# First-chunk q projection of a two-layer attention and SwiGLU kernel: tile 1 averaged by halves, tile 3 transposed by DMA, q's second half in passes of 128 tokens, wo in four loads

## The chip, the core and the metric

The kernel runs on one core of one Trainium2 chip. The metric is device time in microseconds (us) of one execution, as a median over fast runs. Engines are named as in the profile: PE is TensorE's matmul, PEld its weight loads, DVE is VectorE, ACT is ScalarE, POOL is GpSimd, SP is SyncE, which issues most DMAs. L347 is line 347 of the kernel's source. A bank is a buffer that PE's matmuls write into (in PSUM); copying it out is called evacuating it. In the profile's names, x is the input, xn a normalised or centred tile, xnT its transpose, slot a buffer for weights, wo the weights of the output projection, and oT the attention's output.

## The reference, cut to what matters

```
x = x + A(layernorm(x), wqkv, wo)        # attention, 32 heads, window of 8 keys 2 apart
x = x + B(layernorm(x), w1, w3, w2)      # SwiGLU, F = 3584
x = x + A(layernorm(x), wqkv, wo)        # the same weights again
x = x + B(layernorm(x), w1, w3, w2)
```

x is 2048 tokens by 1024, bf16. The kernel works on 4 chunks of 512 tokens, each of 4 tiles of 128 tokens.

## The kernel before

The program records operations (engine, estimated duration, what is read and written) and a list scheduler puts them in order for each engine. For PE it picks among lanes; lane 1 is attention's output projection:

```
def place(self, n_banks=8, rate=330e3):
    ...
            if e == "PE":
                cands = []
                for k, ops in lanes.items():
                    if heads[k] < len(ops) and waiting[ops[heads[k]]] == 0:
                        cands.append(ops[heads[k]])
                times = [(max(free[e], ready_at[o], bank_time(o)), -o.lane, o.seq, o) for o in cands]
    ...
```

The program then gives each engine its instructions in exactly this order, whatever the real durations are.

The edit is in the function that does the first chunk's q projection. Tiles 0 and 1 are centred, transposed on PE and projected while weight rows still arrive; their scaling is applied later. Tiles 2 and 3 are normalised, transposed on PE and projected as q's second half. Tiles 0 and 1 are then also normalised and transposed by DMA, for k and v:

```
def q_first():
    ...
    for j in range(2, TPC):                       # tiles 2 and 3
        stats(j, [("ce", 1, 0)]); root(j, j + 1); apply(j)
        transposed(xn[j], ..., xnT[b][:, :, j * P:(j + 1) * P], ...)     # on PE, through PSUM
    for j in range(2):                            # tiles 0 and 1, for k and v
        ...
        dma(256, xnT[b][:, :, j * P:(j + 1) * P], xn[j][:], ..., transpose=True)
    ...
    wslots[1] = q_weights(1, "s")                 # k: two loads of 1 MB, ready to issue at once
    ...
```

The output projection adds into x, and the feed-forward stage of the same chunk starts from that x. It has to normalise it and to transpose it by DMA before its first matmul:

```
def b_stage(l, c):
    b = ln(c)          # statistics, normalise, 4 DMA transposes into xnT
    ...                # every first matmul reads all of xnT
```

Of the kernel before, what the change touches and what calls it, by code (L numbers as in the profile page):

```python
# [9 lines left out]
ALU = mybir.AluOpType  # L10
# [146 lines left out]
def kernel(  # L157
# [11 lines left out]
    nc = tc.nc  # L169
    P = 128  # L170
# [77 lines left out]
    def dve(dur, emit, reads, writes, cls=2, **kw):  # L248
        return pr.add("DVE", dur, emit, reads, writes, cls, **kw)

    def act(dur, emit, reads, writes, cls=0, **kw):
        return pr.add("ACT", dur, emit, reads, writes, cls, **kw)
# [167 lines left out]
    def transposed(src, keys, dst, dkeys, pieces=((0, 4, "DVE"), (4, 8, "ACT"))):  # L420
        for k0, k1, eng in pieces:
            n = k1 - k0
            add, fn, dur = ((dve, nc.vector.tensor_copy, 0.15 + n * 0.0675) if eng == "DVE" else
                            (act, nc.scalar.copy, 0.2 + n * 0.0975))
            a = Acc()

            def tr(op, a=a, k0=k0, n=n):
                pt = bank[a.bank][:].bitcast(BF16)
                for k in range(n):
                    nc.tensor.transpose(pt[:, k * P:(k + 1) * P], src[:, (k0 + k) * P:(k0 + k + 1) * P], ident[:])  # L430
            tro = pr.add("PE", 0.0625 * n, tr, [keys[k0 // 4], "ident"], [], takes=[a], lag=0.17, lane=2)

            def emit(op, a=a, k0=k0, k1=k1, n=n, fn=fn):
                pt = bank[a.bank][:].bitcast(BF16)
                fn(dst[:, k0:k1, :], pt[:, 0:n * P].rearrange("p (k t) -> p k t", k=n))
            evac(add, dur, emit, tro, [], dkeys[k0:k1], a, cls=-9)

    def q_first():
# [6 lines left out]
        for kk in range(4):  # L445
# [5 lines left out]
        rows[2](7)  # L451
        b, q, stats, root, apply = ln(0, first=True)
        ce = hT[:, 8:16, :]
        dve(0.77, lambda _: nc.vector.tensor_scalar(xn[2][:, 0:512], x_sb[0][:, 0:512], 1.0 / D, 0.0, op0=ALU.mult,
                                                    op1=ALU.add, accum_out=mean[:, 0:1]),
            [("x", 0, 0)], [("xn", 2), ("mean", 0)], -9)
        act(0.82, lambda _: nc.scalar.activation(xn[3][:, 0:512], x_sb[0][:, 512:1024], ACTF.Copy, scale=1.0 / D,
                                                 accum_out=part[:, 0:1]), [("x", 0, 1)], [("xn", 3), ("part", 0)], -9)
        rows[2](6, queue="AQ", after=[("part", 0)])
        act(1.25, lambda _: nc.scalar.activation(xn[3][:], x_sb[1][:], ACTF.Copy, scale=1.0 / D,  # L460
                                                 accum_out=mean[:, 1:2]), [("x", 1, 0), ("x", 1, 1)],
            [("xn", 3), ("mean", 1)], -9)
        for j in range(2):
            for h in range(2):
                c0 = 512 * h
                if j == 0:
                    dve(0.31, lambda _, c0=c0: nc.vector.tensor_scalar(
                        xn[0][:, c0:c0 + 512], x_sb[0][:, c0:c0 + 512], mean[:, 0:1], part[:, 0:1], op0=ALU.subtract,
                        op1=ALU.subtract), [("x", 0, 0), ("x", 0, 1), ("mean", 0), ("part", 0)],
                        [("xn", 0), ("xn", 0, h)], -9)  # L470
                else:
                    dve(0.31, lambda _, c0=c0: nc.vector.tensor_scalar(  # L472
                        xn[1][:, c0:c0 + 512], x_sb[1][:, c0:c0 + 512], mean[:, 1:2], None, op0=ALU.subtract),
                        [("x", 1, 0), ("x", 1, 1), ("mean", 1)], [("xn", 1), ("xn", 1, h)], -9)
            transposed(xn[j], [("xn", j, h) for h in range(2)], ce[:, :, j * P:(j + 1) * P],
                       [("ce", j, k) for k in range(KT)],
                       ((0, 2, "DVE"), (2, 4, "DVE"), (4, 8, "ACT")) if j == 0 else ((0, 4, "DVE"), (4, 8, "ACT")))
        dve(0.16, lambda _: nc.vector.tensor_tensor(mean[:, 0:1], mean[:, 0:1], part[:, 0:1], op=ALU.add),
            [("mean", 0), ("part", 0), ("ce", 1, 0)], [("mean", 0)], -9)
        for j in range(2, TPC):  # L480
            stats(j, [("ce", 1, 0)])
            root(j, j + 1)
            apply(j)
            transposed(xn[j], [("xn", j)] * 2, xnT[b][:, :, j * P:(j + 1) * P],
                       [("xnT", b, j, k // 4) for k in range(KT)])
        for j in range(2):
            act(1.25, lambda _, j=j: nc.scalar.activation(sgt[j][:].rearrange("p a b -> p (a b)"), x_sb[j][:],
                                                          ACTF.Square, bias=mean[:, j:j + 1], scale=-1.0,
                                                          accum_out=part[:, j:j + 1]),
                [("x", j, 0), ("x", j, 1), ("mean", j)] + [("ce", 1, KT - 1)],  # L490
                [("part", j), ("sgt", j, 0), ("sgt", j, 1)], -8)
            act(0.3, lambda _, j=j: nc.scalar.activation(sd[q][:, j:j + 1], part[:, j:j + 1], ACTF.Sqrt, bias=epst[:],
                                                         scale=1.0 / D),
                [("part", j), "eps"], [("sd", q, j)], -8, table="sqrt")
            dve(0.16, lambda _, j=j: nc.vector.reciprocal(rstd[q][:, j:j + 1], sd[q][:, j:j + 1]), [("sd", q, j)],
                [("rstd", q, j)], 0)
            dve(0.5, lambda _, j=j: nc.vector.tensor_scalar(xn[j][:], x_sb[j][:], mean[:, j:j + 1],
                                                            rstd[q][:, j:j + 1], op0=ALU.subtract, op1=ALU.mult),
                [("x", j, 0), ("x", j, 1), ("mean", j), ("rstd", q, j), ("xn", TPC - 1)],
                [("xn", j)] + [("xn", j, h) for h in range(2)], 0)  # L500
            dma(256, xnT[b][:, :, j * P:(j + 1) * P], xn[j][:], [("xn", j)], [("xnT", b, j)], 0, transpose=True)
# [6 lines left out]
        def store(pa, op, j0):  # L508
            for g in range(4):
                evac(act, 0.59, lambda _, a=pa[g], g=g: nc.scalar.copy(  # L510
                    hT[:, 2 * g:2 * g + 2, j0 * P:(j0 + 2) * P],
                    bank[a.bank][:].rearrange("p (m t) -> p m t", m=2)), op[g], [],
                    [("hT", 2 * g + m, j) for m in range(2) for j in (j0, j0 + 1)], pa[g])
# [12 lines left out]
        store(pa, [op] * 4, 0)  # L526
        pa = [Acc() for _ in range(4)]
        ops = []
        for g in range(4):
            lk = [[q_lhs(wslots[0], kk, m)[0] for kk in range(KT)] for m in (2 * g, 2 * g + 1)]  # L530

            def emit(op, g=g, lk=lk, pa=pa):
                for m in range(2):
                    for kk in range(KT):
                        nc.tensor.matmul(bank[pa[g].bank][:, m * 2 * P:(m + 1) * 2 * P], lhsT=lk[m][kk],  # L535
                                         rhs=xnT[b][:, kk, 2 * P:4 * P], start=(kk == 0 and m == 0),
                                         stop=(kk == KT - 1), skip_group_check=True)
            ops.append(pr.add("PE", 16 * 0.1092, emit,
                              [("w", i, k) for i in wslots[0][0] for k in range(4)] +
                              [("xnT", b, j, h) for j in (2, 3) for h in range(2)],  # L540
                              [], takes=[pa[g]], lag=0.17))
        store(pa, ops, 2)
        for m0 in range(0, KT, 2):
            dma(256, spill_view(0, 0, m0, 0), hT[:, m0:m0 + 2, :],
                [("hT", m, j) for m in (m0, m0 + 1) for j in range(TPC)], [("d", 0, 0, 0, m0)], 1)
# [6 lines left out]
        for which, key, tile_ in ((1, "kT", kT), (2, "vT", vT)):  # L552
            dve(0.11, lambda _, tile_=tile_: nc.vector.memset(tile_[:, :, 0:HALO], 0.0), [], [(key, "h")], 1)
            q_tile(0, 0, which, wslots[which], b, (key, tile_))
        for t0, t1_ in ((0, 2), (2, 4), (4, 6), (6, 7), (7, 8)):
            dma(256 * (t1_ - t0), wo[:, t0:t1_, :], wo_v[:, t0:t1_, :], [("d", 0, 2, 0, 6)], [("wo", t0)], 3)
        stage_no[0] += 1

# [24 lines left out]
    def t_stage(l, half):  # L583
# [54 lines left out]
        for j in range(TCH // P):  # L638
            n = tok0 // P + j
            for hh in range(2):  # L640
                a = Acc()
                op = mm8(a, [(oT[oh][:, t, j * P:(j + 1) * P], wo[:, t, hh * 512:(hh + 1) * 512]) for t in range(KT)],
                         True, True, [("oT", oh, t) for t in range(KT)] + [("wo", t) for t in (0, 2, 4, 6, 7)], lane=1)
                xs = x_sb[n][:, hh * 512:(hh + 1) * 512]
                evac(dve, t1(512), lambda _, xs=xs, a=a: nc.vector.tensor_tensor(xs, xs, bank[a.bank][:], op=ALU.add),  # L645
                     op, [("x", n, hh)], [("x", n, hh)], a)
# [126 lines left out]
```

## Time and profile before

| | before |
|---|---|
| median of 3 runs | 1614.96 us |
| span of the profiled run | 1613.1 us |
| PE busy | 99% of the span |
| PE waits, whole run | 1.4 us, all before 7 us |
| first matmul of k (L347) | 21.49 us |

The span runs from the first instruction to the last. A line of the timeline gives the start, the length, the engine, the line, the operation, output and input, the number of instructions merged, and in brackets the idle time before it with what ended it. The lines themselves stand in the prediction.

### The profile page before, as it was taken

Reading aid. Unit: us, or ns where it says so; the run is one execution under the profiler, and the core shown is the slowest. Engines: PE = TensorE matmul, PEld = TensorE weight load, DVE = VectorE, ACT = ScalarE, POOL = GpSimd, SP = SyncE. Lnnn points to the kernel's source line nnn. Section 1 sums busy time; section 2 is a strip of 40 time slices with the busy share of each in tenths; the row PEclk is TensorE's granted clock in tenths of the full one; section 3 lists DMA queues with packets and bytes.
Section 4 is the critical chain, followed back from the end, with each engine's and each line's share of the span. In section 5 each row is a group of like instructions: output and inputs, shape, how many; then the busy total and the mean of one; then the engine's idle time right before and its main releaser. Section 6 shows DMA issues by size and latency. Waiting matters only on the chain.

```text
span 1613.1 us, 19082 instructions
## 1 busy us (share of the span) xinstructions
PE 1601.3 (99%) x7463; PEld 762.7 (47%) x7610; DVE 1122.3 (70%) x1906; ACT 329.6 (20%) x526; POOL 5.3 (0%) x28
## 2 busy tenths in 40 slices
PE   9999999999999999999999999999999999999999
PEld 7555544444444444444444444444444444444444
DVE  5899888988889888898898729884299831211211
ACT  5423322021201222113311032110321101101110
POOL 1000000000000000000000000000000000000000
PEclk9999999999999999999999999999999999999999
DMA  9834755495548764858545487365873464454451
GB/s 321 228 105 151 221 166 171 127 227 158 171 141 253 194 186 137 216 164 251 176 131 163 157 248 228 121 176 174 254 220 118 160 179 156 144 177 149 156 167 42
DMA packets 350649, 285.80 MB, mean 177 GB/s; under 512 B 72288, under 2 KB 344928, under 8 KB 350560
## 3 DMA queue, kind: packets, MB, share of 16 engines
q1 hardware_dynamic: 350128, 283.94, 58.8%
q8 instruction: 59, 0.97, 0.2%
q10 hardware_dynamic: 432, 0.66, 0.1%
q14 instruction: 30, 0.25, 0.1%
HBM read 238.94 MB, written 29.36 MB: 166 GB/s over the span
## 4 chain that ended last, share of the span: by engine, by line
PE 99%; issue 1%; DMA 0%; ACT 0%; DVE 0%; ACTq 0%
PE bank L347 98%; PE bank L535 0%; PE bank L521 0%; DMA x<-in_A_x_dram 0%; PE bank L430 0%; ACT L281 0%; DVE xn L472 0%; ACT xn L460 0%; DVE x L700 0%; ACTq L460 0%
## 5 line engine op out<-in xcount | busy, mean ns | idle before, releaser
L347 PE MATMUL bank<-xnT,slot 128*128 128x512 bf16 x4955 | 1088.7, 379 | 5.3
L347 PEld LDWEIGHTS <-slot 128*128 128x128 bf16 x5056 | 518.2, 102 | 572.9
L347 PE MATMUL bank<-slot,hT 128*128 128x512 bf16 (+2 forms) x1812 | 387.3, 372 | 1.9
L670 DVE TENSOR_TENSOR hT<-sg,bank 128x512 bf16<-128x512 bf16 x224 | 153.4, 685 | 214.4 <-PE bank L347 194.9
L265 DVE TENSOR_TENSOR scr<-scr 128x1024 bf16<-128x1024 bf16 (+3 forms) x576 | 293.4, 539 | 2.0
L347 PEld LDWEIGHTS <-hT 128*128 128x128 bf16 x1848 | 178.5, 98 | 208.7
L668 ACT ACTIVATE sg<-bank 128x512 bf16<-128x512 f32 x224 | 133.7, 597 | 660.5 <-PE bank L347 608.8
L265 DVE TENSOR_TENSOR scr<-qT,kT 128x2048 bf16<-128x2048 bf16 x128 | 154.1, 1219 | 73.3 <-DMA kT<-qkv_d 71.0
L405 ACT CAST sgt<-bank 128x512 bf16<-128x512 f32 x184 | 107.3, 585 | 315.2 <-PE bank L347 300.3
L265 DVE TENSOR_TENSOR scr<-pA,vT 128x2048 bf16<-128x2048 bf16 x128 | 152.5, 1220 | 0.3
L700 DVE TENSOR_TENSOR x<-x,bank 128x512 bf16<-128x512 bf16 (+1 forms) x66 | 43.9, 670 | 121.5 <-PE bank L347 121.4
L347 PE MATMUL bank<-wo,oT 128*128 128x512 bf16 x502 | 112.6, 379 | 0.6
L313 DVE BATCH_NORM_STATS2 st<-x 128x6 f32<-128x512 bf16 x124 | 81.8, 681 | 11.9 <-DMA x<-in_A_x_dram 11.4
L347 PEld LDWEIGHTS <-oT 128*128 128x128 bf16 x512 | 50.1, 98 | 60.3
L645 DVE TENSOR_TENSOR x<-x,bank 128x512 bf16<-128x512 bf16 x64 | 43.9, 687 | 37.0 <-PE bank L347 35.8
L320 ACT ACTIVATE sd<-mv,epst 128x4 f32<-128x4 f32 (+1 forms) x17 | 5.1, 297 | 172.4 <-DVE mv L316 172.1
L628 DVE STREAM_TRANSPOSE pA<-pB 128x2048 bf16<-128x2048 bf16 x16 | 37.0, 2310 | 0.5
L605 DVE STREAM_TRANSPOSE pB<-pA 128x2048 bf16<-128x2048 bf16 x16 | 37.0, 2310 | 0.5
L668 ACT ACT_TABLE_LOAD x20 | 25.7, 1283 | 56.2 <-PE bank L347 56.0
L265 DVE TENSOR_TENSOR pA<-scr 128x256 bf16<-128x256 bf16 x128 | 35.9, 286 | 0.4
L265 DVE TENSOR_TENSOR oT<-scr 128x256 bf16<-128x256 bf16 x128 | 33.9, 288 | 0.1
L327 DVE TENSOR_SCALAR xn<-x,mv,rstd 128x1024 bf16<-128x1024 bf16 x62 | 30.7, 541 | 3.5 <-DMA xnT<-xn 3.4
(61 smaller groups left out, 209.0 us busy)
## 6 DMA issues: line engine op xcount, KB each, us to landing
slot<-in_B_w_dram SPq DMA_DIRECT2D x160, 1024.0 KB, 5.9
slot<-in_A_wqkv_dram SPq DMA_DIRECT2D x28, 1024.0 KB, 5.1
qkv_d<-sgt SPq DMA_DIRECT2D x92, 256.0 KB, 3.3
qT<-qkv_d SPq DMA_DIRECT2D x16, 512.0 KB, 5.7
slot<-in_B_w_dram SPq DMA_DIRECT2D x16, 512.0 KB, 5.7
kT<-qkv_d SPq DMA_DIRECT2D x14, 544.0 KB, 6.7
vT<-qkv_d SPq DMA_DIRECT2D x14, 544.0 KB, 4.9
out_dram<-x SPq DMA_DIRECT2D x31, 128.0 KB, 4.3
```

The lines of the kernel that those rows point to most:

```text
L265: return lambda _: nc.vector.tensor_tensor(o, a, b, op=op)
L313: dve(0.67, lambda _, hh=hh: nc.vector.bn_stats(st[q][:, j, hh, :], x_sb[n][:, hh * 512:(hh + 1) * 512]), [("x", n, hh)] + list(after), [( ...
L320: act(0.3, lambda _: nc.scalar.activation(sd[q][:, j0:j1], mv[q][:, j0:j1, 1], ACTF.Sqrt, bias=epst[:]), [("mv", q, j) for j in range(j0, ...
L327: dve(0.5, lambda _: nc.vector.tensor_scalar(xn[j][:], x_sb[n][:], mv[q][:, j, 0:1], rstd[q][:, j:j + 1], op0=ALU.subtract, op1=ALU.mult), ...
L347: nc.tensor.matmul(bank[a.bank][:, 0:ncol], lhsT=w, rhs=r, start=first and i == 0, stop=last and i == n - 1)
L405: evac(act, 0.59, lambda _, a=a, i=i, m=m: nc.scalar.copy(sgt[i][:, m % 2, :], bank[a.bank][:]), op, [], [("sgt", i, m % 2)], a)
L605: dve(2.31, lambda _: nc.vector.transpose(psmT[:].rearrange("p c d -> p (c d)"), psm[:].rearrange("p w s -> p (w s)")), allA, ["pB"])
L628: dve(2.31, lambda _: nc.vector.transpose(At[:].rearrange("p w s -> p (w s)"), AeT[:].rearrange("p c d -> p (c d)")), ["pB"], allA)
L645: evac(dve, t1(512), lambda _, xs=xs, a=a: nc.vector.tensor_tensor(xs, xs, bank[a.bank][:], op=ALU.add), op, [("x", n, hh)], [("x", n, hh) ...
L668: evac(act, 0.6, lambda _, i=i, a=ag: nc.scalar.activation(sg[i][:], bank[a.bank][:], ACTF.Silu), og, [], [("sg", i)], ag, table="silu")
L670: evac(dve, t1(512), lambda _, i=i, a=au, f=f: nc.vector.tensor_tensor(hT[:, f, :], sg[i][:], bank[a.bank][:], op=ALU.mult), ou, [("sg", i ...
L700: evac(dve, t1(cn), lambda _, xs=xs, a=a, cn=cn: nc.vector.tensor_tensor(xs, xs, bank[a.bank][:, 0:cn], op=ALU.add), op, [("x", n, hh)], [ ...
```

## The change

The intent is to take work off PE in the first 21 us, where it waits and where it does transposes instead of matmuls. Tile 1's mean is formed half on DVE and half on ACT. Tile 3 is transposed by DMA instead of on PE, and so that PE need not wait for it, q's second half goes over tile 2 first and over tile 3 after that. wo comes in four loads instead of five.

```
-        for j in range(2): ...        # tile 1: one ACT sum over 1024, one subtraction operand
+        for j in range(2):
+            dve(0.77, ... tensor_scalar(xn[2][:, 0:512], x_sb[j][:, 0:512], 1.0 / D, ..., accum_out=mean[:, j:j + 1]) ...)
+            act(0.82, ... activation(xn[3][:, 0:512], x_sb[j][:, 512:1024], ..., accum_out=part[:, j:j + 1]) ...)
             ...
-                       ((0, 2, "DVE"), (2, 4, "DVE"), (4, 8, "ACT")) if j == 0 else ((0, 4, "DVE"), (4, 8, "ACT")))
+                       ((0, 2, "DVE"), (2, 4, "DVE"), (4, 8, "ACT")))
         ...
-            transposed(xn[j], [("xn", j)] * 2, xnT[b][:, :, j * P:(j + 1) * P], ...)
+            if j == 2:
+                transposed(xn[j], [("xn", j)] * 2, xnT[b][:, :, j * P:(j + 1) * P], ...)
+            else:
+                dma(256, xnT[b][:, :, j * P:(j + 1) * P], xn[j][:], ..., transpose=True)
         ...
-        for g in range(4):                       # 16 matmuls of 256 columns each
+        for j in (2, 3):
+            for g in range(4):                   # 16 matmuls of 128 columns each
         ...
-        for t0, t1_ in ((0, 2), (2, 4), (4, 6), (6, 7), (7, 8)):
+        for t0, t1_ in ((0, 2), (2, 4), (4, 6), (6, 8)):
             dma(256 * (t1_ - t0), wo[:, t0:t1_, :], ...)
```

More of the change, by code (lines that the diff above doesn't have):

```diff
@@ L453, in q_first @@
         ce = hT[:, 8:16, :]
-        dve(0.77, lambda _: nc.vector.tensor_scalar(xn[2][:, 0:512], x_sb[0][:, 0:512], 1.0 / D, 0.0, op0=ALU.mult,
-                                                    op1=ALU.add, accum_out=mean[:, 0:1]),
-            [("x", 0, 0)], [("xn", 2), ("mean", 0)], -9)
-        act(0.82, lambda _: nc.scalar.activation(xn[3][:, 0:512], x_sb[0][:, 512:1024], ACTF.Copy, scale=1.0 / D,
-                                                 accum_out=part[:, 0:1]), [("x", 0, 1)], [("xn", 3), ("part", 0)], -9)
@@ L459, in q_first @@
-        rows[2](6, queue="AQ", after=[("part", 0)])
-        act(1.25, lambda _: nc.scalar.activation(xn[3][:], x_sb[1][:], ACTF.Copy, scale=1.0 / D,
-                                                 accum_out=mean[:, 1:2]), [("x", 1, 0), ("x", 1, 1)],
-            [("xn", 3), ("mean", 1)], -9)
-        for j in range(2):
-            for h in range(2):
-                c0 = 512 * h
-                if j == 0:
-                    dve(0.31, lambda _, c0=c0: nc.vector.tensor_scalar(
-                        xn[0][:, c0:c0 + 512], x_sb[0][:, c0:c0 + 512], mean[:, 0:1], part[:, 0:1], op0=ALU.subtract,
-                        op1=ALU.subtract), [("x", 0, 0), ("x", 0, 1), ("mean", 0), ("part", 0)],
-                        [("xn", 0), ("xn", 0, h)], -9)
-                else:
-                    dve(0.31, lambda _, c0=c0: nc.vector.tensor_scalar(
-                        xn[1][:, c0:c0 + 512], x_sb[1][:, c0:c0 + 512], mean[:, 1:2], None, op0=ALU.subtract),
-                        [("x", 1, 0), ("x", 1, 1), ("mean", 1)], [("xn", 1), ("xn", 1, h)], -9)
+        for j in range(2):
+            dve(0.77, lambda _, j=j: nc.vector.tensor_scalar(xn[2][:, 0:512], x_sb[j][:, 0:512], 1.0 / D, 0.0,
+                                                             op0=ALU.mult, op1=ALU.add, accum_out=mean[:, j:j + 1]),
+                [("x", j, 0)] + [("ce", 0, 2)] * j, [("xn", 2), ("mean", j)], -9)
+            act(0.82, lambda _, j=j: nc.scalar.activation(xn[3][:, 0:512], x_sb[j][:, 512:1024], ACTF.Copy,
+                                                          scale=1.0 / D, accum_out=part[:, j:j + 1]),
+                [("x", j, 1)], [("xn", 3), ("part", j)], -9)
+            if j == 0:
+                rows[2](6, queue="AQ", after=[("part", 0)])
+            for h in range(2):
+                dve(0.31, lambda _, j=j, c0=512 * h: nc.vector.tensor_scalar(
+                    xn[j][:, c0:c0 + 512], x_sb[j][:, c0:c0 + 512], mean[:, j:j + 1], part[:, j:j + 1],
+                    op0=ALU.subtract, op1=ALU.subtract), [("x", j, 0), ("x", j, 1), ("mean", j), ("part", j)],
+                    [("xn", j), ("xn", j, h)], -9)
@@ L475, in q_first @@
             transposed(xn[j], [("xn", j, h) for h in range(2)], ce[:, :, j * P:(j + 1) * P],
                        [("ce", j, k) for k in range(KT)],
-                       ((0, 2, "DVE"), (2, 4, "DVE"), (4, 8, "ACT")) if j == 0 else ((0, 4, "DVE"), (4, 8, "ACT")))
-        dve(0.16, lambda _: nc.vector.tensor_tensor(mean[:, 0:1], mean[:, 0:1], part[:, 0:1], op=ALU.add),
-            [("mean", 0), ("part", 0), ("ce", 1, 0)], [("mean", 0)], -9)
+                       ((0, 2, "DVE"), (2, 4, "DVE"), (4, 8, "ACT")))
@@ L480, in q_first @@
+        dve(0.16, lambda _: nc.vector.tensor_tensor(mean[:], mean[:], part[:], op=ALU.add),
+            [("mean", j) for j in range(2)] + [("part", j) for j in range(2)] + [("ce", 1, 0)],
+            [("mean", j) for j in range(2)], -9)
         for j in range(2, TPC):
@@ L483, in q_first @@
             apply(j)
-            transposed(xn[j], [("xn", j)] * 2, xnT[b][:, :, j * P:(j + 1) * P],
-                       [("xnT", b, j, k // 4) for k in range(KT)])
+            if j == 2:
+                transposed(xn[j], [("xn", j)] * 2, xnT[b][:, :, j * P:(j + 1) * P],
+                           [("xnT", b, j, k // 4) for k in range(KT)])
+            else:
+                dma(256, xnT[b][:, :, j * P:(j + 1) * P], xn[j][:], [("xn", j)], [("xnT", b, j, h) for h in range(2)],
+                    0, transpose=True)
         for j in range(2):
@@ L489, in q_first @@
                                                           accum_out=part[:, j:j + 1]),
-                [("x", j, 0), ("x", j, 1), ("mean", j)] + [("ce", 1, KT - 1)],
+                [("x", j, 0), ("x", j, 1), ("mean", j), ("xnT", b, 2, 1) if j else ("ce", 1, KT - 1)],
                 [("part", j), ("sgt", j, 0), ("sgt", j, 1)], -8)
@@ L528, in q_first, with emit @@
         ops = []
-        for g in range(4):
-            lk = [[q_lhs(wslots[0], kk, m)[0] for kk in range(KT)] for m in (2 * g, 2 * g + 1)]
-            def emit(op, g=g, lk=lk, pa=pa):
-                for m in range(2):
-                    for kk in range(KT):
-                        nc.tensor.matmul(bank[pa[g].bank][:, m * 2 * P:(m + 1) * 2 * P], lhsT=lk[m][kk],
-                                         rhs=xnT[b][:, kk, 2 * P:4 * P], start=(kk == 0 and m == 0),
-                                         stop=(kk == KT - 1), skip_group_check=True)
-            ops.append(pr.add("PE", 16 * 0.1092, emit,
-                              [("w", i, k) for i in wslots[0][0] for k in range(4)] +
-                              [("xnT", b, j, h) for j in (2, 3) for h in range(2)],
-                              [], takes=[pa[g]], lag=0.17))
-        store(pa, ops, 2)
+        for j in (2, 3):
+            for g in range(4):
+                lk = [[q_lhs(wslots[0], kk, m)[0] for kk in range(KT)] for m in (2 * g, 2 * g + 1)]
+                def emit(op, g=g, lk=lk, pa=pa, j=j):
+                    for m in range(2):
+                        t0 = m * 2 * P + (j - 2) * P
+                        for kk in range(KT):
+                            nc.tensor.matmul(bank[pa[g].bank][:, t0:t0 + P], lhsT=lk[m][kk],
+                                             rhs=xnT[b][:, kk, j * P:(j + 1) * P],
+                                             start=(kk == 0 and m == 0 and j == 2), stop=(kk == KT - 1),
+                                             skip_group_check=True)
+                ops.append(pr.add("PE", 16 * 0.0558, emit,
+                                  [("w", i, k) for i in wslots[0][0] for k in range(4)] +
+                                  [("xnT", b, j, h) for h in range(2)], [], takes=[pa[g]], lag=0.17))
+        store(pa, ops[4:], 2)
         for m0 in range(0, KT, 2):
@@ L642, in t_stage @@
                 op = mm8(a, [(oT[oh][:, t, j * P:(j + 1) * P], wo[:, t, hh * 512:(hh + 1) * 512]) for t in range(KT)],
-                         True, True, [("oT", oh, t) for t in range(KT)] + [("wo", t) for t in (0, 2, 4, 6, 7)], lane=1)
+                         True, True, [("oT", oh, t) for t in range(KT)] + [("wo", t) for t in (0, 2, 4, 6)], lane=1)
                 xs = x_sb[n][:, hh * 512:(hh + 1) * 512]
```

## The prediction

> **What bounds the kernel now.** I read the page of the profile first: the busy shares, then the chain that ended last.
>
> ```profile
> span 1613.1 us, 19082 instructions
> PE 1601.3 (99%) x7463; PEld 762.7 (47%) x7610; DVE 1122.3 (70%) x1906; ACT 329.6 (20%) x526; POOL 5.3 (0%) x28
> PE 99%; issue 1%; DMA 0%; ACT 0%; DVE 0%; ACTq 0%
> ```
>
> TensorE (PE) carries 99% of the span and of the chain; no other engine is near it. So the next view is the list of waits of PE over the whole run, which has three lines in all:
>
> ```profile
> PE bank L285 <- PEq L757: 0.8, 1, 0.8
> PE bank L430 <- DVE xn L472: 0.4, 1, 0.4
> PE bank L521 <- DMA slot<-in_A_wqkv_dram: 0.2, 1, 0.2
> ```
>
> Columns: who waited for whom, total us, times, longest. All of it lies in the first 7 us. From the first matmul of k (line 347, at 21.49 us) PE runs to the end without a wait. The change touches only the first chunk's q projection, before that matmul, and the loads of wo. So the whole question is: **at what time does the first L347 matmul start?** Whatever that start moves, the end moves, unless a new wait appears later.
>
> The timeline of the first 60 us gives the start of every PE stage (start us, length us, engine, line):
>
> ```profile
> 5.19 0.61 PE L521 MATMUL bank<-hT,slot 128*128 128x128 bf16 x8
> 5.96 0.62 PE L521 MATMUL bank<-hT,slot 128*128 128x128 bf16 x8 [0.16 <-DMA slot<-in_A_wqkv_dram]
> 6.96 0.66 PE L430 MATMUL bank<-ident,xn 128*128 128x128 bf16 x8 [0.39 <-DVE xn L472]
> 7.46 5.44 PE L521 MATMUL bank<-hT,slot 128*128 128x128 bf16 x64
> 12.74 1.06 PE L430 MATMUL bank<-ident,xn 128*128 128x128 bf16 x16
> 13.63 1.04 PE L521 MATMUL bank<-hT,slot 128*128 128x256 bf16 x8
> 14.51 7.15 PE L535 MATMUL bank<-xnT,slot 128*128 128x256 bf16 x64
> 21.49 38.80 PE L347 MATMUL bank<-xnT,slot 128*128 128x512 bf16 x175
> ```
>
> The lengths include the last matmul's run-out, so paces are taken from start to start. A 256-column matmul: (21.49 - 14.51)/64 = 0.109 us. The group at 7.46 holds 32 matmuls of 128 columns and 32 of 256 (from the order of instructions); 12.74 - 7.46 = 5.28, less 32 x 0.109 = 3.49, leaves 1.79, or 0.056 us for a 128-column matmul. The transposes at 12.74 agree: (13.63 - 12.74)/16 = 0.056.
>
> Last, the DMA side, since the change puts a transpose there. From the timeline of the DMA-issuing queue, the issues by line, and the table of windows (window, PE, PEld, DVE, ACT, POOL busy, clock, DMA share, GB/s):
>
> ```profile
> 13.41 1.36 SPq L259 DMA_TRANSPOSE xnT<-xn  x1
> 14.87 3.07 SPq L259 DMA_TRANSPOSE xnT<-xn  x1
> ...
> slot<-in_A_wqkv_dram SPq DMA_DIRECT2D x1, 1024.0 KB, 10.4
> xnT<-xn SPq DMA_TRANSPOSE x1, 5.6
> xnT<-xn SPq DMA_TRANSPOSE x1, 5.0
> ...
> 16.75:17.75 1.00, 1.00 (x11) 0.90 (x10) 0.00 (x0) 0.29 (x1) 0.18 (x1) 1.00 0.43 30
> 18.00:19.25 1.25, 1.25 (x14) 1.13 (x12) 0.00 (x0) 0.58 (x1) 0.00 (x0) 1.00 1.28 287
> ```
>
> The last number of an issue line is us from issue to landing. k's second weight load was issued at 7.72 and landed at 7.72 + 10.4 = 18.1. The two transposes (tiles 0 and 1 in this kernel) landed at 13.41 + 5.6 = 19.0 and 14.87 + 5.0 = 19.9, although the first was issued well before. Between 16.75 and 17.75 the DMAs moved only 30 GB/s: most engines were through with the weights and the transpose did not go on until the last part of the weights was in. Its bulk moved from 18.0.
>
> **What the Trainium skill says.** "DMA: Bandwidth & Descriptors", section "Queues, rings and completion order": on each DMA engine descriptors are consumed in ring order. This trace agrees: 18.1, 19.0, 19.9 land in the order of issue. "TensorE: Matmul & The Clock Gate", "Back-to-back issue gap": about 81 ns per 128-column matmul in a stream with weight loads, 56 ns for the isolated gap. The trace decides for 56 although every matmul here has its own weight load. "VectorE: DVE Perf Modes", "The three transpose paths": 390 ns on TensorE and 1309 ns by DMA for 128x128. Here eight TensorE transposes in a row cost 16 x 0.056 / 2 = 0.45 us of PE, and a lone DMA transpose of eight such blocks (at 40.72 us) took 3.3 us from issue to landing.
>
> **The change part by part.**
>
> Tile 1 by halves. Before, ScalarE summed all of tile 1 (L460, 1.06 + 0.19 from 5.37) and VectorE could subtract only at 6.55. After, VectorE sums one half (0.69 + 0.08) beside ScalarE's other half (0.63 + 0.19), from about 5.37, so both are done near 6.2. The subtraction now has two scalars, as tile 0's: 0.41 instead of 0.35 us. First half ready near 6.65, 0.3 us earlier. The changed order of instructions puts weight row 2 of tile 0 (8 x 0.056 = 0.45 us) ahead of tile 1's transposes, so they start when that is done, at about 6.6 (row 2 landed: issued 2.13, some 4.4 to landing) + 0.45 = 7.05. Tile 0 needed 5.19 - 4.53 = 0.66 us from its first transpose to its first matmul, with the same two-block evacuations; so tile 1's matmuls start near 7.7, its three rows take 24 x 0.056 = 1.34, and the 256-column part starts near 9.05. Before, it started at 7.46 + 1.79 = 9.25. Gain **0.2 us**.
>
> Tile 3's transposes off PE. 8 x 0.056 = **0.45 us** saved. Four rows of 8 x 0.109 take 3.49 to 12.54, tile 2's transposes 0.45 to 12.99, the last row 0.87 to 13.86. Second half of q, tile 2: its copies sit behind other VectorE work, as before (13.29 to 13.7), and are no wait. It starts at 13.86.
>
> Second half in passes of 128. 64 matmuls of 256 become 128 of 128: 128 x 0.056 = 7.17 against 6.98, a cost of **0.2 us**. Tile 2's pass ends at 13.86 + 3.58 = 17.44. Without a wait the k matmuls would start at 21.03, or 0.46 us earlier than before.
>
> The DMA transpose of tile 3. Its input is normalised at about 12.9 (before, 12.31 + 0.55), it is the first transpose on the queue, and it stands behind the same 2 MB of k weights as before. Issued at 12.9 instead of 13.41, it gains nothing: in the kernel before the first transpose waited for the weights that landed at 18.1, not for its issue. So I take its landing from there: **19.0 us**. Tile 3's pass waits on that semaphore; PE stands from 17.44 to 19.05, **1.6 us**, and the 0.65 us won before it only lengthen this wait. Then 64 x 0.056 = 3.58 to 22.63. Against 21.49 that is **+1.14 us**.
>
> Tiles 0 and 1, needed by k, come 0.9 to 1.3 us apart behind it: near 19.9 and, with an issue that opens at about 18.0 and the 3.3 us of a lone transpose, 21.3. k starts at 22.63, so they are hidden. ScalarE takes tile 1's square later, but tile 1 is then ready by about 16.7, before its issue opens.
>
> The wo loads: one DMA issue (0.44 us of the issuing queue) less at 57 us; no PE wait is near. Zero. The matmuls from L347 on are the same 7416 in number; the eight-matmul groups of the output projection come 8 to 24 places later in the first part of the run, which gives VectorE more room, not less. Zero.
>
> Sum: 1614.96 + 1.14 = 1616.1 us.
>
> **The rivals.** (1) The transpose lands in time (by 17.4): then the 0.46 us of savings show, 1614.5. For it: the gap at 16.75 to 17.75 is a tail, perhaps of one slow engine, and might be shorter; against it: even without that tail the weights end near 16.75, and 0.9 us of transpose plus 0.6 us of completion give 18.2, still 0.8 late, for about 1615.3. (2) The third transpose becomes the last: if the issue of each one stalls as the 3.07 us one did, tile 1's lands after 22.6 and k waits more: about 1617. For it: that 3.07; against: in the later group of four at 49.31 to 55.9 no issue after the second is that long in what I saw. (3) Weight loads bound the short matmuls: PEld shows 0.098 us each; at that pace each pass takes 6.3 us, tile 3's would end near 26.4 after tile 2's at 20.1, and the kernel takes 1620. Against: the measured 0.056. (4) The reordered bulk makes a wait somewhere: +1 to 3 us; against: 1590 us without one before, and groups moved later.
>
> **Range and chances.** I give 65% to the main path, 15% to (1) and its half-way form, 12% to (2), the rest to (3) and (4). Runs of before spread over 0.4 us. Range 1614.6 to 1617.2. Two per cent are 32 us, which nothing here reaches: the whole stage touched is 21 us.
>
> **What would show it.** The list of PE's waits should have a new line, L535 for a DMA of xnT, about 1.6 us; the timeline should show L535 in two groups of 64, the second from about 19.05, and the first L347 near 22.6; from there no wait, so the same length to the end. The wait on L472 should be gone and the one before tile 1's transposes under 0.2. I am wrong if L535 does not wait, if the first L347 starts before 21.5, or if waits appear after it.

## The result and the profile after

| | before | after |
|---|---|---|
| median, 6 runs each | 1615.05 us | 1617.64 us |
| range | 1614.86 to 1615.52 | 1617.45 to 1617.91 |
| span of the profiled run | 1613.1 us | 1616.0 us |
| first matmul of k (L347) | 21.49 us | 22.72 us |

The ratio is 1.0016 (95% interval 1.0003 to 1.0029). Ratios here are the mean time of one kernel's fast runs over that of the other's of the same rounds, so not quite the ratio of the medians quoted. The difference is far under two per cent, but the interval leaves out 1. The kernel became 2.6 us slower, where 1.1 had been predicted; the time lies above the range.

From the page of the changed kernel, its span, its busy shares and its chain by engine:

```profile
span 1616.0 us, 19187 instructions
PE 1601.7 (99%) x7519; PEld 763.2 (47%) x7666; DVE 1121.7 (69%) x1908; ACT 327.6 (20%) x524; POOL 4.9 (0%) x28
...
PE 98%; DMA 1%; DVE 1%; issue 1%; SPq 0%
```

PE's busy time is the same within 0.4 us. The chain now passes through DMA and DVE for some time. So PE waits more, and the list of its waits in the changed kernel (who for whom: total us, times, longest) says for what:

```profile
PE bank L347 <- DMA xnT<-xn: 1.7, 1, 1.7
PE bank L535 <- DMA xnT<-xn: 1.1, 1, 1.1
...
PE bank L519 <- DMA slot<-in_A_wqkv_dram: 0.4, 2, 0.2
```

The second line was predicted, at 1.6 us. The first was not. The timeline of the changed kernel around the first of the two waits:

```profile
8.18 4.99 PE L519 MATMUL bank<-hT,slot 128*128 128x128 bf16 x56
...
14.33 3.74 PE L535 MATMUL bank<-xnT,slot 128*128 128x128 bf16 x64
19.15 3.73 PE L535 MATMUL bank<-xnT,slot 128*128 128x128 bf16 x64 [1.08 <-DMA xnT<-xn]
22.72 22.62 PE L347 MATMUL bank<-xnT,slot 128*128 128x512 bf16 x101
```

L535 now comes in two passes, and the second starts at 19.15, 0.1 us from the predicted 19.05. The first L347 starts at 22.72 (predicted 22.63), 1.23 us later than before.

The other wait is far from the edit. The timeline of PE around the second half of the first chunk's output projection (input wo,oT) and the first feed-forward stage, first in the kernel before:

```profile
166.53 7.07 PE L347 MATMUL bank<-wo,oT 128*128 128x512 bf16 x31
173.44 14.84 PE L347 MATMUL bank<-xnT,slot 128*128 128x512 bf16 x67
```

and in the changed kernel:

```profile
169.50 7.07 PE L347 MATMUL bank<-wo,oT 128*128 128x512 bf16 x31
176.41 12.25 PE L347 MATMUL bank<-xnT,slot 128*128 128x512 bf16 x55
190.33 1.02 PE L347 MATMUL bank<-xnT,slot 128*128 128x512 bf16 x4 [1.68 <-DMA xnT<-xn]
```

After the output projection PE has q, k and v work of the last chunk to do, then it starts the feed-forward stage of chunk 0. In between, x has to be normalised and transposed. That takes nearly the same time in both: the last of the four transposes landed 20.4 us after the output projection began before the change, 20.7 after. But PE's filling work lasts 64 matmuls before and only 56 after, since the output projection stands 8 matmuls later in PE's order (after 648 other full-width matmuls, not 640). Eight matmuls of 0.2158 us are 1.73 us. Before, the transposes landed at 186.91 and the stage began near 166.53 + 96 x 0.2158 = 187.25, so they were 0.3 us early. After, PE stands 1.68 us: the 1.73, less those 0.3, plus the 0.3 by which they now came later.

The two add up: 1.23 + 1.68 = 2.91 us, and the spans differ by 1616.0 - 1613.1 = 2.9 us. This is the account of these two profiles; the medians differ by 2.59. PE's first transposes began at 4.53 us in the profile of before, and at 4.73 to 5.32 in all others, so some tenths of the 1.23 may belong to that profile and not to the change.

### The profile page after: what moved, and what is told of

Its sections match the earlier page's. It is cut to its first block, busy times and chain, and to the rows that moved or that the text cites. A ratio compares the mean times of both kernels' runs of the same rounds, so it can differ in the third digit from the quotient of the medians.

```text
span 1616.0 us, 19187 instructions
## 1 busy us (share of the span) xinstructions
PE 1601.7 (99%) x7519; PEld 763.2 (47%) x7666; DVE 1121.7 (69%) x1908; ACT 327.6 (20%) x524; POOL 4.9 (0%) x28
## 4 chain that ended last, share of the span: by engine, by line
PE 98%; DMA 1%; DVE 1%; issue 1%; SPq 0%
PE bank L347 97%; DMA xnT<-xn 1%; DVE scr L265 0%; PE bank L519 0%; DMA slot<-in_A_wqkv_dram 0%; PE bank L535 0%; DVE xn L327 0%; SPq L261 0%; DVE x L645 0%; DVE st L313 0%; DVE pA L265 0%; DVE hT L435 0%; DVE x L700 0%; PE bank L430 0%; DVE mv L316 0%
## 5 line engine op out<-in xcount | busy, mean ns | idle before, releaser
L347 PE MATMUL bank<-xnT,slot 128*128 128x512 bf16 x4955 | 1089.0, 379 | 7.0 <-DMA xnT<-xn 1.7
L347 PEld LDWEIGHTS <-slot 128*128 128x128 bf16 x5056 | 518.0, 102 | 574.9 <-issue 2.1
L347 PE MATMUL bank<-slot,hT 128*128 128x512 bf16 (+2 forms) x1812 | 387.3, 372 | 1.9
L347 PEld LDWEIGHTS <-hT 128*128 128x128 bf16 x1848 | 178.5, 98 | 208.7
L347 PE MATMUL bank<-wo,oT 128*128 128x512 bf16 x502 | 112.4, 379 | 0.5
L347 PEld LDWEIGHTS <-oT 128*128 128x128 bf16 x512 | 50.2, 98 | 60.2
```

What stands on the lines that cost most here:

```text
L347: nc.tensor.matmul(bank[a.bank][:, 0:ncol], lhsT=w, rhs=r, start=first and i == 0, stop=last and i == n - 1)
```

## The experiments

Two theories were left open by the traces. For the wait at 190 us: PE's order alone makes it, or the rival, DVE and the DMAs are later in the changed kernel for reasons of their own. For the wait at 19 us: what keeps the transpose that long. All eight kernels gave correct results; each was timed in five rounds beside the kernel before, in two sets of four (before: 1615.11 and 1615.08 us, medians of 9 runs each).

### Tile 3's part alone

The kernel before, with tile 3's DMA transpose, the passes of 128 and the wait of tile 1's square on ACT for tile 2's copy that goes with them; tile 1 and wo as before.

```
+            if j == 2:
+                transposed(...)
+            else:
+                dma(256, xnT[b][:, :, j * P:(j + 1) * P], xn[j][:], ..., transpose=True)
+        for j in (2, 3):
+            for g in range(4): ...
```

> Only tile 3's DMA transpose and the passes of 128; tile 1 and wo as before. Theory (the first wait is set by the landing of tile 3 behind k's weights, the second by the output projection placed 8 matmuls later): both waits are there as in the changed kernel, L535 waits 1 to 1.4 us for the transpose, the first L347 starts at 22.6 to 22.8, one wait of L347 of about 1.7 us near 190 us, time 1617.4 to 1617.8. Rival (tile 1 by halves or wo in four loads moves the bulk of the program): the wait near 190 us is gone and the time is near 1616.2.

Measured: 1617.27 us (1616.94 to 1617.59), ratio 1.0013 (1.0 to 1.0025). Its waits of PE, as above:

```profile
PE bank L541 <- DMA xnT<-xn: 1.5, 1, 1.5
PE bank L347 <- DMA xnT<-xn: 0.9, 1, 0.9
```

L541 is here the line of L535. Both waits are there, and the output projections stand after 392 and 648 other matmuls, as in the changed kernel. The first wait is 0.1 us over the expected range, the second 0.8 us under its value, as the last transpose landed 19.9 us after the output projection began and not 20.7; the total is just below the range. So tile 3's part carries nearly all of the loss, 2.2 of the 2.6 us; the other 0.4 is no more than the spread of these runs. Adding the halves and wo leaves the output projections at the same places.

### The output projections held where they were

The changed kernel; only for the first chunk's two output projections, PE's lane is chosen by a fixed count of other full-width groups of 8 matmuls (48 and 80, the places of the kernel before; the changed kernel has 49 and 81).

```
+                    due = outs < len(pin) and full >= pin[outs]          # pin = [48] * 4 + [80] * 4
                     for k, ops in lanes.items():
+                        if outs < len(pin) and (k == 1 and not due or k == 0 and due):
+                            continue
```

> The changed kernel, with the first chunk's two output projections held in TensorE's order where the kernel before had them (after 384 and 640 other full-width matmuls, not 392 and 648). Theory (the second wait comes from the order alone: the attention output was ready 3.3 and 5.5 us before those matmuls): L535's wait of 1.1 us stays, the wait of L347 near 190 us falls from 1.7 to under 0.3 us, time 1616.0 to 1616.4. Rival (VectorE or the DMA transposes after it are late by themselves, since VectorE runs 2.7 us behind the kernel before at 72 us): PE waits at the output projection or still 1.5 us near 190 us, time 1617.4 to 1617.8.

Measured: 1616.07 us (1615.83 to 1616.2), ratio 1.0005 (0.9993 to 1.0018). Its waits of PE, without the one at the start of the run, and the same stretch of PE's timeline (all lines are shifted by the edit: L544 is L535, L354 is L347):

```profile
PE bank L544 <- DMA xnT<-xn: 1.2, 1, 1.2
...
PE bank L528 <- DMA slot<-in_A_wqkv_dram: 0.3, 1, 0.3
```

```profile
167.83 7.07 PE L354 MATMUL bank<-wo,oT 128*128 128x512 bf16 x32
174.74 16.57 PE L354 MATMUL bank<-xnT,slot 128*128 128x512 bf16 x76
```

There is no wait behind the output projection any more, and none before it: DVE's last write of the attention output ended 3.75 us before it, so the attention was not late. The kernel won 1.6 us against the changed kernel's 1617.64 (another set of runs) and is 0.96 us over the kernel before, which leaves the first wait. By medians this wait so costs about 1 us, and not quite the 1.23 of the two profiles.

### The kernel before with its output projections moved

The converse: the same edit on the kernel before, with counts 49 and 81. Nothing else was edited.

> The kernel before, with only the first chunk's two output projections held 8 matmuls later in TensorE's order (after 392 and 648 others, as the changed kernel has them). Theory (that order alone makes the second wait): nothing changes before 104 us, and one new wait of L347 for a transpose appears near 188 us, of 8 x 0.2158 = 1.73 us less the 0.3 us that the transposes were early before, so 1.3 to 1.5 us; time 1616.3 to 1616.7. Rival (the wait needs the later loads and the later VectorE of the changed kernel): no wait, time 1614.9 to 1615.3.

Measured: 1617.13 us (1616.65 to 1617.38), ratio 1.0012 (0.9999 to 1.0024). PE's timeline at that place (L354 is L347):

```profile
175.55 12.25 PE L354 MATMUL bank<-xnT,slot 128*128 128x512 bf16 x56
189.46 2.75 PE L354 MATMUL bank<-xnT,slot 128*128 128x512 bf16 x12 [1.66 <-DMA xnT<-xn]
```

The wait appears without any other part of the change, at 1.66 us. The expected size was 1.3 to 1.5, and the time is above the range too: 2.05 us over the kernel before, of which the wait explains 1.66. In the profiled run the first L347 came at 21.87, 0.38 us later than in the profile of before, with nothing changed in that stretch: its first transposes started at 5.32 instead of 4.53 us. That start differs by some tenths from profile to profile here, and effects of that size are not read from one profile.

### The passes of 128 alone

The kernel before with the second half of q in passes of 128 tokens, and tile 3 still transposed on PE.

```
+        for j in (2, 3):
+            for g in range(4): ...            # 16 matmuls of 128 columns
```

> The kernel before, with the second half of q in passes of 128 tokens alone; tile 3 still transposed on TensorE. Theory: 128 matmuls at 0.056 for 64 at 0.109 cost 0.2 us, the first L347 starts at 21.7, no wait of L535, time 1615.1 to 1615.4. Rival (short matmuls with their own weight load run at 0.08 us or more): first L347 at 24 or later, time 1618.

Measured: 1615.28 us (1615.18 to 1615.56), ratio 1.0001 (0.9988 to 1.0013). PE's timeline (L537 is L535):

```profile
14.67 7.31 PE L537 MATMUL bank<-xnT,slot 128*128 128x128 bf16 x128
21.81 3.41 PE L347 MATMUL bank<-xnT,slot 128*128 128x512 bf16 x15
```

From start to start (21.81 - 14.67)/128 = 0.0558 us per matmul, each with its own weight load. The passes cost 0.2 us, as expected. The first chunk's output projections stay after 384 and 640 other matmuls, so it is the DMA transpose of tile 3, and not the passes, that moves them in the scheduler's order.

### k's weights on another queue

The changed kernel with k's two loads issued by ACT instead of SP, once tile 1's copy is made.

```
-        wslots[1] = q_weights(1, "s")
+        wslots[1] = q_weights(1, "s", after=[("ce", 1, KT - 1)], queue="AQ")
```

> The changed kernel, with k's two weight loads issued from ScalarE's queue at about 10 us, so tile 3's transpose no longer stands behind them in the same queue. Theory (the transpose waits for the weights ahead of it in its queue): issued at about 13.2 it lands by 17.5 instead of 19.1, L535 waits under 0.4 us, the first L347 starts at 21.1 to 21.7; the wait near 190 us stays at 1.7 us, time 1616.2 to 1616.8. Rival (a transpose behind 5 us of full traffic takes about 6 us in any queue, since the engines are shared): it lands near 19, the time stays 1617.4 to 1617.8.

Measured: 1617.76 us (1617.7 to 1617.92), ratio 1.0016 (1.0002 to 1.003). The loads went out at 8.40 and 8.83 us, not at 10; the first went out while ACT's copy of tile 1, from 8.13 to 8.71, still ran. The transpose was issued at 13.18. First, PE's wait for it; then the queues that moved data (packets, MB, share of 16 engines) from 13.5 to 15.5 us; then the same from 15.5 to 17.5; then the issue of that transpose with its us to landing:

```profile
PE bank L535 <- DMA xnT<-xn: 1.0, 1, 1.0
...
q10 hardware_dynamic: 373, 0.76, 102.0%
...
q1 hardware_dynamic: 487, 0.12, 113.0%
q10 hardware_dynamic: 125, 0.23, 32.7%
...
xnT<-xn SPq DMA_TRANSPOSE x1, 5.8
```

The theory fell: the transpose landed at 13.18 + 5.8 = 19.0 as ever. In the first 2 us every data packet belongs to ACT's queue (q10). SP's queue (q1) moved nothing, though the transpose had been issued on it and nothing else was ahead of it there. Part of this silence is the transpose's own: in the next run, where the DMAs were idle from 14.25, its first packet came 1.3 us after its issue (14.96 after 13.68); here it came 2.5 us after (15.69). In the next 2 us both queues moved packets. The transpose moves 128 x 1024 x 2 bytes in packets of about 256 bytes (0.12 MB in 487), so some 1024 in all, and about half had gone by 17.75. The rest followed only then, about when the last weights were in (they landed at 17.94). The other runs with both loads in flight show the same: 505 to 524 such packets by 17.75, and a landing between 18.89 and 19.48, whether the first transpose was issued at 13.15 or at 14.17. So it is not the place in one queue that makes it wait, but the traffic of the 16 DMA engines.

The other wait stayed, 1.8 us before the L347 at 190.29. The list of waits puts it down to DVE, but the last transpose landed at 190.15, as close before it as in the changed kernel.

### k's second weights behind the transposes

The changed kernel, with k's second load ready to issue only when tile 0's input to its transpose is written. It then goes out behind the transposes of tiles 3 and 0.

```
-                dma(1024, v, ..., after, ...)
+                dma(1024, v, ..., list(after) + list(late) * h, ...)
-        wslots[1] = q_weights(1, "s")
+        wslots[1] = q_weights(1, "s", late=[("xn", 0)])
```

> The changed kernel, with k's second 1 MB of weights issued after tile 3's and tile 0's transposes instead of before them. Theory (tile 3's transpose can't finish before the slowest DMA engine has moved its share of the weights that were issued earlier, on whichever queue): with 1 MB less ahead, it lands at 16.4 to 17.2 instead of 19.1 and L535 does not wait. The wait moves to k: its second weights and tile 1's transpose now land at 21.5 to 22.7, so the first L347 starts at 21.6 to 22.8, no earlier than in the kernel before; the wait near 190 us stays 1 to 1.7 us, time 1616.5 to 1617.8. Rival (the transpose is slow by itself, near 6 us at this place): it lands at 18.5 or later and L535 still waits 1 us.

Measured: 1618.21 us (1617.93 to 1619.99), ratio 1.0022 (1.001 to 1.0035). Tile 3's issue with its us to landing, PE's timeline, and two windows (window, then PE, PEld, DVE, ACT, POOL busy, clock, DMA share, GB/s):

```profile
xnT<-xn SPq DMA_TRANSPOSE x1, 3.4
...
14.63 7.31 PE L535 MATMUL bank<-xnT,slot 128*128 128x128 bf16 x128
23.97 1.27 PE L347 MATMUL bank<-xnT,slot 128*128 128x512 bf16 x5 [2.03 <-issue]
...
14.25:14.75 0.50, 0.50 (x8) 0.46 (x7) 0.14 (x1) 0.50 (x2) 0.00 (x0) 1.00 0.00 0
15.00:16.00 1.00, 1.00 (x22) 1.00 (x20) 0.00 (x0) 1.00 (x3) 0.00 (x0) 1.00 1.10 207
```

With 1 MB less ahead of it, the transpose took 3.4 us instead of 5.9 and landed at 17.05; PE ran both passes without a stop. So the weights in flight were what held it. Two of the five runs, 1619.55 and 1619.99 us at a clock of 0.999, took over 1.3 us longer than the other three (1617.93 to 1618.21), for a reason not found; the loss does not rest on them. The DMAs stood still from 14.25 to 14.75, and PE waited 2.0 us before k: tile 1's transpose, now behind the second weights, landed at 23.88. That is later than the 22.8 us expected at most, and the total is 0.4 us above its range. The later wait was 0.8 us here, as the last transpose landed 19.8 us after the output projection began.

### Tile 1 by halves alone

The kernel before with the first part of the change only.

> The kernel before, with tile 1 averaged and evacuated by halves alone; tile 3 on TensorE, second half of q in passes of 256. Theory (the halves bring tile 1 forward by some 0.3 us, but its third piece takes one PSUM bank more, which tile 3's transposes need): the wait of L472 is gone, but a wait of 0.5 to 1.2 us appears between tile 3's transposes and L529, the first L347 starts at 21.6 to 22.6, and, as the second output projection stands 8 matmuls earlier, no wait near 188 us: time 1615.2 to 1616.3. Rival (halves are a gain by themselves): first L347 at 21.2 to 21.3, time 1614.7 to 1614.9.

Measured: 1615.65 us (1615.29 to 1615.89), ratio 1.0003 (0.9989 to 1.0017). PE's timeline at q's second half (L529 is L535):

```profile
14.15 0.61 PE L430 MATMUL bank<-ident,xn 128*128 128x128 bf16 x8
15.18 7.15 PE L529 MATMUL bank<-xnT,slot 128*128 128x256 bf16 x64 [0.42 <-DVE xnT L435]
```

Tile 3's transposes, at 14.15, now stand behind the last row of q's first half instead of ahead of it, apparently because the scheduler had no PSUM bank for them earlier, and L529 waits 0.42 us for the copy, a little under the 0.5 expected at least. So the halves are not a gain by themselves; in the changed kernel this wait is absent, as tile 3's transposes are gone. That the bank is what moved them was argued from the order; with one bank fewer taken, in the next run, they are back in their old place, as one group of 16 at 13.29 us.

### Tile 1 averaged by halves, evacuated in two pieces

As the last, but with `((0, 4, "DVE"), (4, 8, "ACT"))` kept for tile 1, so that no bank more is taken.

> The kernel before, with tile 1 averaged by halves on VectorE and ScalarE, but still evacuated in two pieces, so no bank more. Theory: TensorE's wait for tile 1 (0.2 to 0.4 us in the kernel before) shrinks and nothing else changes; first L347 at 21.2 to 21.5, time 1614.8 to 1615.1, a gain of 0 to 0.3 us that may be within the spread. Rival (the third row of tile 0, now ahead of tile 1's transposes, leaves TensorE idle while tile 1's four-block copy is made): a wait of 0.3 us behind tile 1's transposes, time 1615.1 to 1615.4.

Measured: 1615.22 us (1615.18 to 1615.53), ratio 1.0001 (0.9988 to 1.0013). PE's timeline:

```profile
7.10 0.62 PE L515 MATMUL bank<-hT,slot 128*128 128x128 bf16 x8 [0.53 <-DVE xn L464]
...
8.46 4.99 PE L515 MATMUL bank<-hT,slot 128*128 128x128 bf16 x56 [0.29 <-DVE hT L435]
```

The rival was right about the 0.29 us behind tile 1's transposes. But the theory's gain did not come either: PE's wait ahead of them did not shrink from 0.4 us, it was 0.53. The list names DVE for it; the matmuls that waited, at 7.10, read weight row 2, which landed at 7.05. The time can't be told from the kernel before. No version beat it. What tile 3 in time could win is at most the 0.46 us worked out in the prediction, of which 0.2 are the halves' gain that no run showed; that is less than half of the 1.14 us at which the prediction put the landing's cost.

## Why the prediction was wrong

- **What bounds the kernel** held: PE at 99%, and the end moves with PE's waits alone. The sum 1.23 + 1.68 = 2.91 accounts for the 2.9 us of the spans.
- **Tile 1 by halves** failed, without effect on the time. The gain of 0.2 us did not come: weight row 2, now ahead of tile 1's transposes, landed at 7.03 us and not at 6.6, PE waited 0.4 us for rows, and the 256-column part started at 8.18 + 24 x 0.056 = 9.52, not at 9.05. Without the halves (tile 3's part alone) PE reached tile 2's pass at 14.16, before the changed kernel's 14.33. Since PE then waits for tile 3, this cost nothing. Alone the halves gave nothing either.
- **The passes of 128** held: 0.2 us, at 0.0558 us per matmul.
- **The DMA transpose of tile 3** held in its numbers: landing 19.1 against 19.0, first L347 at 22.72 against 22.63. PE stood 1.1 us and not 1.6: it reached the first pass at 14.33 and not at 13.86, as its first transposes began 0.2 us later in this profile and it waited 0.4 us for weight rows, and the profile counts the last matmul's run-out as busy. The reason given was too narrow. It spoke of the order in the ring, and landings in the order of issue don't show that: the run with k's weights on ACT's queue has the same landing without it, and the run with 1 MB less in flight shows that the traffic itself holds it. "Its bulk moved from 18.0" is half true: in the kernel before, 507 packets of 256 bytes had moved by 17.25, half of what one transpose has.
- **The step that failed** is the last one before the sum: "the eight-matmul groups of the output projection come 8 to 24 places later in the first part of the run, which gives VectorE more room, not less. Zero." It asked only who feeds the output projection, and not who waits for it. Its result goes through DVE and four DMA transposes to the feed-forward stage, and in the kernel before that path arrived only 0.3 us before it was needed. Moved by one group, 1.73 us, and landing 0.3 us later after it, it became a wait of 1.7 us where "zero" had been forecast. The rival named it ("the reordered bulk makes a wait somewhere") and set it aside with the same wrong reason, "groups moved later". The two runs with fixed places show it both ways: taken back, the wait is gone; put into the kernel before, it appears.

Open: why the second half of a transpose comes only after the last of the loads in flight, in whichever queue they are; why the last of the four transposes landed between 19.6 and 21.7 us after the output projection began, from run to run; and why the scheduler's estimates move the output projections by one group when tile 3 goes to the DMA. Only that they do was seen.

## What to carry to other kernels

Where a scheduler of your own sets the order, compare the order of the whole program after a local edit, and for each moved group ask what it waits for and also what waits for it: the slack on the consumer's side may be a fraction of one group. A DMA transpose issued behind 2 MB of loads landed here about 1 us after them (19.0 after 17.9), on the same queue or another; take its landing from an issue in the same place, not from a lone one. A part that frees a bounding engine wins nothing if what takes the work over lands later than the engine would have needed.

## What the Trainium skill lacked or had wrong

- "DMA: Bandwidth & Descriptors", "Queues, rings and completion order", says that each DMA engine takes turns between the queues it has work for, packet by packet. It does not say how a transpose fares in this. Issued on SP's queue at 13.18 us, beside loads on ACT's queue, one moved no packet from 13.5 to 15.5; from 15.5 to 17.5 both queues moved packets (487 and 125), but its second half came only after 17.75. The trace agrees that both queues are served in one stretch; it does not tell the DMA engines apart, so turns within one engine are not shown.
- "Advanced Engine Details and Errata", "X-Bar Transpose (TRN2)", expects 350 to 400 GB/s and transposes as fast as plain DMAs. Here the windows show 287 GB/s (two transposes queued, kernel before) and 207 (one transpose, no weights in the way), against 386 for plain loads from 15 to 16 us in the kernel before.
- "TensorE: Matmul & The Clock Gate", "Back-to-back issue gap", gives about 81 ns for 128-column matmuls in a stream with weight loads. 128 of them, each with its own weight load, took 55.8 ns each here.
- No page of those read gives how long a DMA transpose of 128x1024 takes behind other traffic: 3.4 us with the engines nearly free, 5.6 to 6.2 us behind 2 MB of loads when issued at 13.15 to 13.41 us.
